# Attention with a routed FFN: the last 64 keys move from a chunk's thirteenth slot to its eighth

## The chip, the cores and the metric

One Trainium2 chip, one of its cores. The metric is the device time of the whole program in microseconds (us); a kernel's time is the median of its runs.

## The reference

Eight batches of 3136 tokens. `z` has 64 columns, `u` and `v` have 256.

```python
scores = scale * np.matmul(z, z.transpose(0, 2, 1))     # 8 x 3136 x 3136, scale = 1/3136
attn = np.maximum(scores, 0.0) ** 2
x = u * np.matmul(attn, v)
...
scores = np.einsum('bsd,d->bs', x, w_gate)
top_idx = np.argpartition(-scores[b], capacity)[:capacity]   # 128 tokens of each batch
h = np.maximum(x[b, top_idx] @ w1, 0.0)
out[b, top_idx] = x[b, top_idx] + sigmoid(scores[b, top_idx]) * (h @ w2)
```

The attention is nearly all of the work. Its scores are symmetric: the square for query i and key j is also the one for query j and key i.

## The kernel before

**Tiling.** The queries of a batch go in seven chunks: five of 512, one of 256, one of 320 (`chunks_of`, line 32). The keys are 24 tiles of 128 and a rest of 64. A chunk is worked off in 13 slots (`SLOTS`, line 108): twelve **pair slots** of two key tiles, and one **rest slot** for the 64 last keys. The list `slots` (lines 319 to 338) holds all 8 x 7 x 13 of them in the order in which they run. A pair is *new* when its scores are computed, or *old* when its squares are fetched, transposed, from an earlier chunk that computed them; old and new pairs are spread evenly over a chunk. Before the change the rest slot is the thirteenth of every chunk.

**A slot's work.** Values are split into a high and a low part of type fp32r, so that a product takes several matmuls. For a new pair, `scores` (line 426) issues four score matmuls on PE into one of two PSUM buffers (`sc`, line 440), a ReLU and a square on ACT (L450, the tile `a`; L451, the tile `hi`), and another full square of `a`, on DVE (L462) or on ACT (L456), as counters of estimated busy time choose. `low` (line 466) transposes the squares on DVE for later chunks (L483, L503) and makes the low part `lo` on POOL or DVE (L518), by the same counters. For an old pair ACT makes the high part from the fetched tile `qk` (L418), and the low part is again L518. The rest slot has two score matmuls, half the ACT work, and three short DVE operations on 64 partitions (L462, L474, L483); its high and low parts share one tile.

`mix` (line 526) then multiplies: a pair slot issues twelve matmuls (eight with `hi`, four with `lo`, line 556), a rest slot four with `hi` and `Vr`. They add up in two PSUM banks `acc`, one for each half of the 256 columns of `v`. There are three such banks, so a chunk's second half takes the bank that held the first half of the chunk before. In between, after `turn` matmuls, `mix` calls `more_scores(k + LEAD)`: scores are issued three slots ahead.

**The order.** Each engine's instructions run in the order in which the code issues them. At an edge between chunks stands `finish` (line 594): two DVE operations (L601) read the two banks and so release them; the transposes of the result, a product on POOL (L622) and a sum on DVE follow in later slots. The slot ahead of a rest slot issues its scores after four matmuls, not eight, and only squares the scores (`square_scores`) where it otherwise also makes the low parts; the rest of its work is held to the next slot (lines 1502 to 1505). The first slot of a chunk is sorted by half, so that the second half's bank is needed late (line 549). Routing and FFN of a batch run as tasks in the chunks of the next one.

**Loads.** All large transfers are issued from SP's queue in program order: fetches of old squares (`fetch`, lines 377 to 398; two pairs each, into one of three `qk` tiles, seven slots ahead of their use, lines 1338 to 1346), the next batch's `v` (`stage_v`, line 279), stores of squares and of the result. In the last chunk of a batch ACT and POOL also split the next batch's `v` into its parts (`prep_v`, line 294, L125 and L126), at slots fixed from the end of the batch (lines 1321 to 1330).

Of the kernel before, what the change touches and what calls it, by code (L numbers as in the profile page):

```python
# [25 lines left out]
LATE = 4  # L26
# [62 lines left out]
def attention_then_routed_ffn(ctx: ExitStack, tc: tile.TileContext, zt, ut, v, wg, w1, w2, cst, cst16, keys, outs, at, cap):  # L89
    nc = tc.nc  # L90
    B, S, D = v.shape
# [4 lines left out]
    NCH = len(CHUNKS)  # L96
    WHOLE = NCH - 2
    NK = D // P
    NJ = S // P
# [6 lines left out]
    ROUNDS = 32 // BITS  # L106
    SHARES = P >> BITS
    SLOTS = NJ // 2 + 1

    const = ctx.enter_context(tc.tile_pool(name="const", bufs=1))  # L110
    vpool = ctx.enter_context(tc.tile_pool(name="vpool", bufs=NJ // 2))
# [107 lines left out]
    V = {}  # L219
# [96 lines left out]

    slots = []
    for b in range(B):  # L320
        for c in range(NCH):
            known = min(c, WHOLE) * GT + (2 if c > WHOLE and b < B - 1 else 0)
            old = [(2 * g, 2 * g + 1) for g in range(known // 2)]
            new = [(2 * g, 2 * g + 1) for g in range(known // 2, NJ // 2)]
            if c == WHOLE and b < B - 1:
                new.reverse()
            if c < WHOLE and (b or c):

                new.insert(len(new) - 2, new.pop(1))
            wait = 0.5 if (b, c) == (0, 1) else 0.0  # L330
            both = [(wait + (1 - wait) * (i + 0.5) / len(old), 0, js, True) for i, js in enumerate(old)]
            place = [(i + 0.5) / len(new) for i in range(len(new))]
            if b < B - 1 and c == NCH - 1:
                place = [1.6 / len(old)]
            both += [(x, 1, js, False) for x, js in zip(place, new)]
            slots += [(b, c, js, is_old) for _, _, js, is_old in sorted(both)]
            slots.append((b, c, (NJ,), False))
    assert len(slots) == B * NCH * SLOTS

    squares = [  # L340
# [25 lines left out]
    near = deque()  # L366
# [159 lines left out]
    def mix(k, beside, between):  # L526
# [2 lines left out]
        b, c, js, _ = slots[k]  # L529
        assert k in parts  # L530
        hi, lo = parts.pop(k)
        first, last = k % SLOTS == 0, js[0] == NJ
        if first:
            acc[b, c] = [ps_a.tile([P, CH], F32, name="acc", tag="acc")[:, : CHUNKS[c][1]] for _ in range(NK)]
        ac = acc[b, c]
        todo = []
        if last:
            for h in range(NK):
                for w in range(2):
                    todo.append((h, V[b, NJ][:, w, h], hi[:, 0], w == 1))  # L540
        else:
            for h in range(NK):
                for q, j in enumerate(js):
                    for w in range(2):
                        todo.append((h, V[b, j][:, w, h], hi[:, q], False))
            for q, j in enumerate(js):
                for h in range(NK):
                    todo.append((h, V[b, j][:, 0, h], lo[:, q], False))
            if first and (b or c):
                todo.sort(key=lambda x: x[0])  # L550
        turn = (6 if c else 4) if first else 4 if last or len(slots[min(k + 1, len(slots) - 1)][2]) == 1 else 8
        done, lead, started = 0, 2, set()
        for n, (h, w, mov, stop) in enumerate(todo):
            if n == turn:
                between()
            nc.tensor.matmul(ac[h], w, mov, start=first and h not in started, stop=stop)  # L556
            started.add(h)
            upto = len(beside) * max(0, n - lead + 1) // (len(todo) - lead)
            for op in beside[done:upto]:
                op()  # L560
            done = max(done, upto)
        if turn == len(todo):
            if last:
                near.extend(finish(b, c))
            between()

    gate = {}
# [882 lines left out]
    for k, (b, c, js, is_old) in enumerate(slots):  # L1450
# [48 lines left out]
        now = settle_scores  # L1499
        posts = [*posts[:half], now, *posts[half:]]  # L1500
        held_posts = []
        if k + 2 < len(slots) and len(slots[k + 1][2]) == 1:

            now = square_scores if c < WHOLE and (b or c) else settle_scores
            posts, held_posts = [now], [fn for fn in posts if fn is not settle_scores]
# [9 lines left out]
        clock += took  # L1515
        if tasks:
            ready = max(told + 0.5, clock + 2.0)
        if len(js) == 1 and cap > 0:
            if c == NCH - 1 - late:
                far.extend([None, *route(b)])  # L1520
            elif c >= NCH - late:
# [64 lines left out]
```

## Time and profile before

| | |
|---|---|
| three runs, median (range) | 2067.78 us (2067.12 to 2067.83) |
| the profiled execution's own time | 2067.41 us |
| its span | 2065.6 us |
| PE busy | 2055.2 us (99%) |
| weight loads (PEld) busy | 1744.5 us (84%) |
| DVE, ACT, POOL busy | 1529.0 us (74%), 1291.2 us (63%), 1357.5 us (66%) |
| DMA share of the busiest queue | 70.9% |

The span runs from the first to the last instruction; the profiled execution's time is 1.8 us more than that. Matmuls are pipelined, and their ends are modelled: a row of PE shows 0.39 us for a matmul, while the next one starts 0.23 us later. So PE's busy share tells little; what tells is the distance between the starts of matmuls, and the waits of the weight loads that go ahead of them, which the profile lists apart as PEld.

### The profile page before, as it was taken

What the parts mean: (1) busy time and instruction counts of PE and PEld (TensorE: products, weight loads), DVE (VectorE), ACT (ScalarE), POOL (GpSimd) and SP (SyncE); (2) the same over time, 40 slices, a digit from 0 to 9 for tenths busy, and PEclk for the clock granted to TensorE, in tenths of its full rate; (3) what the DMA queues carried; (4) which work ended last, traced back from release to release, by engine and by line L of the source; (5) the groups of instructions that cost most, each with busy time, mean ns of one, the idle gap of its engine ahead of it and who ended that gap; (6) DMA issues with size and microseconds to landing.
All of it is one profiled execution on the core that took longest, in us unless ns stands there. A gap on an engine that the chain in (4) does not pass through costs nothing.

```text
span 2065.6 us, 31660 instructions
## 1 busy us (share of the span) xinstructions
PE 2055.2 (99%) x10280; PEld 1744.5 (84%) x10280; DVE 1529.0 (74%) x2667; ACT 1291.2 (63%) x1629; POOL 1357.5 (66%) x728
## 2 busy tenths in 40 slices
PE   9999999999999999999999999999999999999999
PEld 6888988889888898888988889888898888888788
DVE  7676678856788667875678756887578876787776
ACT  7665576656775467664676546765477654775543
POOL 6766587756876468764677647875578755765643
PEclk9999999999999999999999999999999999999999
DMA  6788767886668765787767877678776776666862
GB/s 197 207 232 226 217 188 207 233 231 190 193 188 232 212 205 177 199 233 210 208 185 193 235 203 217 184 192 236 194 222 188 192 201 178 206 192 164 213 173 95
DMA packets 442758, 415.52 MB, mean 201 GB/s; under 512 B 133792, under 2 KB 374880, under 8 KB 439520
## 3 DMA queue, kind: packets, MB, share of 16 engines
q1 hardware_dynamic: 441456, 411.01, 70.9%
q0 software_dynamic: 768, 2.10, 0.3%
q8 instruction: 80, 1.31, 0.3%
q14 instruction: 86, 0.70, 0.1%
q10 hardware_dynamic: 368, 0.39, 0.1%
HBM read 238.78 MB, written 174.60 MB: 200 GB/s over the span
## 4 chain that ended last, share of the span: by engine, by line
PE 87%; DVE 3%; issue 2%; ACT 2%; DMA 2%; POOL 1%; SPq 1%; POOLq 0%; DVEq 0%; ACTq 0%
PE acc L556 73%; PE sc L440 12%; ACT hi L451 1%; POOL lo L518 1%; ACT a L450 1%; DVE a L462 1%; DVE aT L483 1%; PE h L1215 1%; PE y L1259 1%; DMA vst<-in_v 0%; DMA squares<-aT 0%; DVE lo L518 0%; DMA qk<-in_zt 0%; PE spread L680 0%; DMA qk<-squares_narrow 0%
## 5 line engine op out<-in xcount | busy, mean ns | idle before, releaser
L556 PE MATMUL acc<-hi,V 128*128 128x512 f32 (+2 forms) x5376 | 1218.4, 364 | 0.5
L518 POOL TENSOR_TENSOR lo<-a,hi 128x1024 fp32r<-128x1024 f32 (+2 forms) x326 | 717.9, 2204 | 563.5 <-DVE a L462 426.7
L556 PEld LDWEIGHTS acc<-hi,V 128*128 128x128 f32 x5376 | 932.9, 188 | 157.4 <-DVE ut L601 5.5
L556 PE MATMUL acc<-lo,V 128*128 128x512 f32 (+2 forms) x2688 | 664.0, 363 | 1.0 <-POOL lo L518 1.0
L450 ACT ACTIVATE a<-sc 128x1024 f32<-128x1024 f32 (+4 forms) x401 | 358.2, 893 | 449.2 <-PE sc L440 421.0
L556 PEld LDWEIGHTS acc<-lo,V 128*128 128x128 f32 x2688 | 471.1, 188 | 76.7 <-POOL lo L518 4.4
L462 DVE TENSOR_TENSOR a<-sc,a 128x1024 f32<-128x1024 f32 (+5 forms) x306 | 307.4, 1005 | 249.8 <-ACT hi L451 225.8
L418 ACT CAST hi<-qk 128x1024 fp32r<-128x1024 f32 (+2 forms) x327 | 279.7, 860 | 220.1 <-PE acc L556 198.1
L483 DVE STREAM_TRANSPOSE aT<-a 128x512 f32<-128x512 f32 (+3 forms) x541 | 349.5, 681 | 76.7 <-ACT a L456 54.4
L451 ACT ACTIVATE hi<-a 128x1024 fp32r<-128x1024 f32 (+4 forms) x401 | 372.2, 928 | 24.8 <-PE acc L556 2.3
L518 DVE TENSOR_TENSOR lo<-qk,hi 128x1024 fp32r<-128x1024 f32 (+2 forms) x220 | 319.2, 1459 | 81.7 <-ACT hi L418 79.3
L440 PE MATMUL sc<-Z,ZH 128*128 128x512 f32 (+2 forms) x746 | 275.1, 373 | 2.3 <-DVE a L462 2.1
L440 PE MATMUL sc<-Z,ZL 128*128 128x512 f32 (+2 forms) x746 | 273.3, 370 | 0.1
L518 POOL TENSOR_TENSOR lo<-qk,hi 128x1024 fp32r<-128x1024 f32 (+2 forms) x107 | 210.0, 1965 | 51.3 <-ACT hi L418 41.6
L440 PEld LDWEIGHTS sc<-Z,ZH 128*128 128x128 f32 x746 | 140.5, 188 | 31.7 <-DVE a L462 6.0
L440 PEld LDWEIGHTS sc<-Z,ZL 128*128 128x128 f32 x746 | 140.5, 188 | 24.7 <-DVE ZL L126 0.5
L126 POOL TENSOR_TENSOR V<-vst,V 128x512 fp32r<-128x512 f32 x92 | 136.5, 1489 | 29.8 <-ACT V L125 26.4
L622 POOL TENSOR_TENSOR ut<-x,w_run 128x1024 f32<-128x1024 f32 (+2 forms) x52 | 126.0, 2422 | 24.4 <-DVE x L613 23.4
L456 ACT ACTIVATE a<-a 128x1024 f32<-128x1024 f32 x93 | 98.8, 1062 | 2.9
L126 POOL TENSOR_TENSOR ZL<-zst,ZH 128x512 fp32r<-128x512 f32 (+2 forms) x56 | 84.2, 1508 | 2.5 <-ACT ZH L125 2.2
L125 ACT CAST V<-vst 128x512 fp32r<-128x512 f32 x95 | 57.9, 609 | 35.5 <-DMA vst<-in_v 35.5
L601 DVE SCALAR_TENSOR_TENSOR ut<-acc,ut 128x512 f32<-128x512 f32 (+2 forms) x112 | 63.9, 611 | 19.5 <-PE acc L556 19.2
(187 smaller groups left out, 1083.1 us busy)
## 6 DMA issues: line engine op xcount, KB each, us to landing
squares<-aT SPq DMA_DIRECT2D x160, 512.0 KB
qk<-squares SPq DMA_DIRECT2D x320, 256.0 KB
squares_narrow<-aT SPq DMA_DIRECT2D x320, 128.0 KB
qk<-squares_narrow SPq DMA_DIRECT2D x80, 512.0 KB
out<-x SPq DMA_DIRECT2D x162, 128.0 KB
ut<-in_ut SPq DMA_DIRECT2D x40, 512.0 KB
vst<-in_v SPq DMA_DIRECT2D x158, 128.0 KB
squares_own<-aT SPq DMA_DIRECT2D x39, 256.0 KB
```

The source lines that it names most:

```text
L126: (lo_on or nc.vector.tensor_tensor)(lo, src, hi.bitcast(F32), op=ALU.subtract)
L418: nc.scalar.copy(by(hi), src)
L440: nc.tensor.matmul(ps[:, q], z[:, j * P : (j + 1) * P], mov, start=z is ZH, stop=z is ZL)
L450: nc.scalar.activation(a, ps[:, :n], AF.Relu)
L451: nc.scalar.activation(pieces[0][0](hi), pieces[0][1], AF.Square)
L456: nc.scalar.activation(a, a, AF.Square)
L462: square = lambda: nc.vector.tensor_tensor(a[rows], of[rows, :n], a[rows], op=ALU.mult)
L483: nc.vector.transpose(to, a[rows, q].rearrange("p (m t a) -> p m t a", m=GT, a=Q))
L518: on.tensor_tensor(view(lo), src, view(hi).bitcast(F32), op=ALU.subtract)
L556: nc.tensor.matmul(ac[h], w, mov, start=first and h not in started, stop=stop)
L601: nc.vector.scalar_tensor_tensor(xT[:, h, :w], acc[b, c][h], SCALE * SCALE, xT[:, h, :w], op0=ALU.mult, op1=ALU.mult)
L622: nc.gpsimd.tensor_tensor(wx, runs, consts["wg_run"].rearrange("p (o r) -> p o r", o=1).broadcast_to([P, NB, RUN]), op=ALU.mult,)
```

## The change

In chunks other than a batch's first, and other than the last batch's four last ones (`inside`), the rest slot is put in as the eighth of thirteen; a pair slot is then the last. So 44 of the 56 chunks change. The code that asked for "a rest slot" where it meant "the last slot of a chunk" now asks for the place. A last slot that is a pair has its matmuls sorted by half, as the first slot has (four with `hi` and two with `lo` of half one, then those of half two), and `finish` is called behind its twelfth matmul. Ahead of a rest slot that lies inside a chunk, the work after the slot is no longer cut down to squaring.

```diff
--- before.py
+++ after.py
@@ -106,6 +106,7 @@
     ROUNDS = 32 // BITS
     SHARES = P >> BITS
     SLOTS = NJ // 2 + 1
+    MIDDLE = SLOTS // 2 + 1
 
     const = ctx.enter_context(tc.tile_pool(name="const", bufs=1))
     vpool = ctx.enter_context(tc.tile_pool(name="vpool", bufs=NJ // 2))
@@ -316,6 +317,10 @@
 
 
 
+    def inside(b, c):
+
+        return c > 0 and c < (NCH if b < B - 1 else NCH - LATE)
+
     slots = []
     for b in range(B):
         for c in range(NCH):
@@ -333,8 +338,9 @@
             if b < B - 1 and c == NCH - 1:
                 place = [1.6 / len(old)]
             both += [(x, 1, js, False) for x, js in zip(place, new)]
-            slots += [(b, c, js, is_old) for _, _, js, is_old in sorted(both)]
-            slots.append((b, c, (NJ,), False))
+            mine = [(b, c, js, is_old) for _, _, js, is_old in sorted(both)]
+            mine.insert(MIDDLE if inside(b, c) else len(mine), (b, c, (NJ,), False))
+            slots += mine
     assert len(slots) == B * NCH * SLOTS
 
     squares = [
@@ -529,15 +535,15 @@
         b, c, js, _ = slots[k]
         assert k in parts
         hi, lo = parts.pop(k)
-        first, last = k % SLOTS == 0, js[0] == NJ
+        first, last, rest = k % SLOTS == 0, k % SLOTS == SLOTS - 1, js[0] == NJ
         if first:
             acc[b, c] = [ps_a.tile([P, CH], F32, name="acc", tag="acc")[:, : CHUNKS[c][1]] for _ in range(NK)]
         ac = acc[b, c]
         todo = []
-        if last:
+        if rest:
             for h in range(NK):
                 for w in range(2):
-                    todo.append((h, V[b, NJ][:, w, h], hi[:, 0], w == 1))
+                    todo.append((h, V[b, NJ][:, w, h], hi[:, 0], last and w == 1))
         else:
             for h in range(NK):
                 for q, j in enumerate(js):
@@ -545,10 +551,10 @@
                         todo.append((h, V[b, j][:, w, h], hi[:, q], False))
             for q, j in enumerate(js):
                 for h in range(NK):
-                    todo.append((h, V[b, j][:, 0, h], lo[:, q], False))
-            if first and (b or c):
+                    todo.append((h, V[b, j][:, 0, h], lo[:, q], last and q == 1))
+            if first and (b or c) or last:
                 todo.sort(key=lambda x: x[0])
-        turn = (6 if c else 4) if first else 4 if last or len(slots[min(k + 1, len(slots) - 1)][2]) == 1 else 8
+        turn = (6 if c else 4) if first else 4 if rest or len(slots[min(k + 1, len(slots) - 1)][2]) == 1 else 8
         done, lead, started = 0, 2, set()
         for n, (h, w, mov, stop) in enumerate(todo):
             if n == turn:
@@ -559,9 +565,9 @@
             for op in beside[done:upto]:
                 op()
             done = max(done, upto)
+        if last:
+            near.extend(finish(b, c))
         if turn == len(todo):
-            if last:
-                near.extend(finish(b, c))
             between()
 
     gate = {}
@@ -1499,7 +1505,7 @@
         now = settle_scores
         posts = [*posts[:half], now, *posts[half:]]
         held_posts = []
-        if k + 2 < len(slots) and len(slots[k + 1][2]) == 1:
+        if k + 2 < len(slots) and len(slots[k + 1][2]) == 1 and not inside(b, c):
 
             now = square_scores if c < WHOLE and (b or c) else settle_scores
             posts, held_posts = [now], [fn for fn in posts if fn is not settle_scores]
@@ -1515,7 +1521,7 @@
         clock += took
         if tasks:
             ready = max(told + 0.5, clock + 2.0)
-        if len(js) == 1 and cap > 0:
+        if k % SLOTS == SLOTS - 1 and cap > 0:
             if c == NCH - 1 - late:
                 far.extend([None, *route(b)])
             elif c >= NCH - late:
```

A rest slot in the middle changes the counters that choose engines. Over the whole program 23 squares go from ACT to DVE (L456: 93 before, 70 now; L462 with 128x1024: 186 before, 209 now), and some low parts change between POOL and DVE.

**PE at the edge between two batches.** The last chunk's slots have 320 columns, the next batch's first chunk 512; `Vr` is the part of `v` of the last 64 keys. Before, the end of the fourth batch:

```order
L440 MATMUL sc<-Z,ZL 128x512
L556 MATMUL acc<-lo,V 128x320 x4
L556 MATMUL acc<-hi,V 128x320 x4
L440 MATMUL sc<-Z,ZH 128x512
L440 MATMUL sc<-Z,ZL 128x512
L440 MATMUL sc<-Z,ZH 128x512
L440 MATMUL sc<-Z,ZL 128x512
L556 MATMUL acc<-hi,V 128x320 x4
L556 MATMUL acc<-lo,V 128x320 x4
L556 MATMUL acc<-hi,Vr 128x320 x4
L440 MATMUL sc<-Z,ZH 128x512
```

The same edge in the changed kernel:

```order
L446 MATMUL sc<-Z,ZL 128x512
L562 MATMUL acc<-lo,V 128x320 x4
L562 MATMUL acc<-hi,V 128x320 x8
L446 MATMUL sc<-Z,ZH 128x512
L446 MATMUL sc<-Z,ZL 128x512
L446 MATMUL sc<-Z,ZH 128x512
L446 MATMUL sc<-Z,ZL 128x512
L562 MATMUL acc<-lo,V 128x320 x4
L562 MATMUL acc<-hi,V 128x320 x4
L562 MATMUL acc<-lo,V 128x320 x2
L562 MATMUL acc<-hi,V 128x320 x2
L446 MATMUL sc<-Z,ZH 128x512
```

The first row of each is the end of the scores of the next chunk's first pair. Behind the last row shown come three more score matmuls and the edge, in the changed kernel with four more `acc` matmuls between them. So from the first row to the edge stood 20 `acc` matmuls and two groups of four score matmuls; now it is 28 and two. The second group, of the second pair, has 16 `acc` matmuls behind it where it had 12. The matmuls of the last slot come half by half.

**ACT in a batch's last chunk.** `V<-vst` splits the next batch's `v`, `Z<-ZH` and `Z<-ZL` prepare queries, `hi<-qk` is the high part of an old pair. Before:

```order
L125 CAST V<-vst 128x512
L271 CAST Z<-ZH 64x512
L271 CAST Z<-ZL 64x512
L418 CAST hi<-qk 128x2x320
L125 CAST V<-vst 128x512
L418 CAST hi<-qk 128x2x320 x2
```

Now:

```order
L126 CAST V<-vst 128x512
L272 CAST Z<-ZH 64x512
L272 CAST Z<-ZL 64x512
L424 CAST hi<-qk 128x2x320
L126 CAST V<-vst 128x512
L424 CAST hi<-qk 128x2x320 x2
```

The order on ACT stays. On PE the four `Vr` matmuls now stand ahead of the tenth slot, which uses the `hi` that follows the casts of `Z`; before, that slot had nine pair slots ahead of it, and now eight and the rest slot.

**SP's queue at the start of that chunk.** `squares_narrow_3` and `_4` are the sources of the fourth and the fifth fetch of the chunk, `vst` is the next batch's `v`. Before:

```order
L394 DMA qk<-squares_narrow_2_113 128x4x256
L397 DMA qk<-squares_narrow_2_113 128x256
L394 DMA qk<-squares_narrow_3_115 128x4x256
L397 DMA qk<-squares_narrow_3_115 128x256
L288 DMA vst<-in_v 32x4x256 x4
L394 DMA qk<-squares_narrow_4_117 128x4x256
L397 DMA qk<-squares_narrow_4_117 128x256
L288 DMA vst<-in_v 32x4x256 x4
```

Now:

```order
L400 DMA qk<-squares_narrow_2_113 128x4x256
L403 DMA qk<-squares_narrow_2_113 128x256
L289 DMA vst<-in_v 32x4x256 x4
L400 DMA qk<-squares_narrow_3_115 128x4x256
L403 DMA qk<-squares_narrow_3_115 128x256
L400 DMA qk<-squares_narrow_4_117 128x4x256
L403 DMA qk<-squares_narrow_4_117 128x256
L289 DMA vst<-in_v 32x4x256 x4
```

The fourth fetch goes out a slot later, behind the first load of `v`.

## Rows read from the trace of the kernel before

**Rows 1.** Page, span and section 1: busy time of each engine

```profile
span 2065.6 us, 31660 instructions
...
PE 2055.2 (99%) x10280; PEld 1744.5 (84%) x10280; DVE 1529.0 (74%) x2667; ACT 1291.2 (63%) x1629; POOL 1357.5 (66%) x728
```

**Rows 2.** Waits of PEld, 250 to 1815 us: total, times, longest

```profile
PEld acc L556 <- DVE ut L601: 4.1, 9, 0.5
PEld acc L556 <- POOL lo L518: 3.9, 11, 1.1
PEld sc L440 <- DVE a L462: 3.0, 9, 0.7
```

**Rows 3.** Timeline (start, us, what), PE, second batch, entry to third chunk

```profile
346.45 0.39 PE L440 MATMUL sc<-Z,ZH 128*128 128x512 f32 x1
...
347.35 1.07 PE L556 MATMUL acc<-hi,V 128*128 128x512 f32 x4
349.12 0.73 PE L556 MATMUL acc<-lo,V 128*128 128x512 f32 x2 [0.69 <-POOL lo L518]
```

**Rows 4.** Timeline of PE, fifth batch, entry to its first chunk

```profile
1024.66 1.08 PE L556 MATMUL acc<-hi,V 128*128 128x512 f32 x4
1025.61 0.50 PE L440 MATMUL sc<-Z,ZH 128*128 128x512 f32 x1
...
1026.64 0.63 PE L556 MATMUL acc<-lo,V 128*128 128x512 f32 x2
1027.33 1.19 PE L556 MATMUL acc<-hi,V 128*128 128x512 f32 x4
1028.35 0.61 PE L556 MATMUL acc<-lo,V 128*128 128x512 f32 x2
```

**Rows 5.** Timeline of DVE at the same entry

```profile
1024.33 1.23 DVE L462 TENSOR_TENSOR a<-sc,a 128x1024 f32<-128x1024 f32 x1
1025.59 1.31 DVE L483 STREAM_TRANSPOSE aT<-a 128x512 f32<-128x512 f32 x2
1026.82 0.85 DVE L601 SCALAR_TENSOR_TENSOR ut<-acc,ut 128x320 f32<-128x320 f32 x2
```

**Rows 6.** Timeline of PE, fourth batch, last chunk

```profile
1013.75 1.34 PE L556 MATMUL acc<-hi,V 128*128 128x320 f32 x8
1014.93 0.75 PE L556 MATMUL acc<-lo,V 128*128 128x320 f32 x4
1015.63 1.43 PE L556 MATMUL acc<-hi,V 128*128 128x320 f32 x8
```

**Rows 7.** Timeline of DVE, fourth batch, end of the second chunk

```profile
852.38 0.69 DVE L462 TENSOR_TENSOR a<-sc,a 64x512 f32<-64x512 f32 x1
...
853.72 0.71 DVE L483 STREAM_TRANSPOSE aT<-a 64x512 f32<-64x512 f32 x1
```

**Rows 8.** Timeline of POOL at the same place

```profile
855.76 2.40 POOL L518 TENSOR_TENSOR lo<-a,hi 128x1024 fp32r<-128x1024 f32 x1 [3.60 <-DVE a L462]
```

**Rows 9.** Groups by form, square on DVE: xcount, busy us, mean ns

```profile
L462 DVE TENSOR_TENSOR a<-sc,a 128x1024 f32<-128x1024 f32 x186 | 227.3, 1222 | 191.5 <-ACT hi L451 169.3 <-issue 20.9
```

**Rows 10.** Busy us (instructions), fourth batch, second chunk: PE PEld DVE ACT POOL

```profile
814.60:857.20 42.60, 42.60 (x191) 35.28 (x190) 40.53 (x98) 29.70 (x32) 29.86 (x15) 1.00 0.58 171
```

**Rows 11.** Timeline of DVE, fourth batch, middle of the second chunk

```profile
834.10 0.84 DVE L814 STREAM_TRANSPOSE ge<-own 32x32 f32<-32x32 f32 x4
```

**Rows 12.** Timeline of ACT, fourth batch, last chunk

```profile
1013.06 0.62 ACT L125 CAST V<-vst 128x512 fp32r<-128x512 f32 x1 [2.26 <-DMA vst<-in_v]
...
1014.85 0.73 ACT L418 CAST hi<-qk 128x640 fp32r<-128x640 f32 x1
```

**Rows 13.** Timeline of SP's queue, start of that chunk

```profile
1001.18 1.76 SPq L288 DMA_DIRECT2D vst<-in_v  x4
```

**Rows 14.** Groups by form: the low of 128x640 on POOL

```profile
L518 POOL TENSOR_TENSOR lo<-qk,hi 128x640 fp32r<-128x640 f32 x12 | 23.5, 1970 | 0.0
...
L518 POOL TENSOR_TENSOR lo<-a,hi 128x640 fp32r<-128x640 f32 x9 | 14.2, 1577 | 47.9 <-DVE a L462 42.5 <-PE old L1065 5.4
```

## Prediction, made before the changed kernel ran

> **What bounds the kernel now.** The page comes first: PE is busy 2055.2 us of a span of 2065.6 [rows 1]. The other engines have a quarter of their time free or more, so PE's own stream sets the end, and moving work among them pays only where PE stops. The reader should not conclude from 99% that only 10 us are to be had: a matmul's row is longer than its distance to the next. So I read the waits of the weight loads next. Between 250 and 1815 us, that is in batches two to seven and at the entries to batches two to eight, they name three things that PE waits for: the release of an `acc` bank by L601, 4.1 us in 9 waits; a low part from POOL, 3.9 us in 11; and the square on DVE that frees a score buffer, 3.0 us in 9 [rows 2]. All three would be small change in another kernel; here they are what is left.
>
> The timeline of PE shows what a wait costs the stream. The pace is four matmuls of 512 columns in 0.90 us, 0.226 each (346.45 to 347.35). In the second batch's third chunk the first `lo` matmul was due at 347.35 + 0.90 = 348.25 and starts at 349.12: 0.87 us lost [rows 3]. At the entry to the fifth batch the scores that start at 1025.61 take until 1026.64, 1.03 us for four: 0.13 lost. The second half's first matmul was due at 1026.64 + 0.45 = 1027.09 and starts at 1027.33, and its four take 1.02 instead of 0.90: 0.24 + 0.12 = 0.36 lost [rows 4]. Both places are the first slot of a chunk, right behind a rest slot.
>
> **The change, part by part.** No matmul is added or removed, so the sum is made of stops that go and stops that come.
>
> *Bank release.* DVE ran the second pair's square at 1024.33, its transposes at 1025.59, and only then L601, at 1026.82 [rows 5]. In the new order the scores of the next chunk's first two pairs are issued eight and four `acc` matmuls earlier before the edge (the order of PE above), 1.2 and 0.6 us at 0.147 us for 320 columns (eight in 1.18 us, from 1013.75 to 1014.93) [rows 6]. ACT takes the first pair, then the second, so DVE's chain starts about 1.0 us earlier. L601 then starts near 1025.8 and its first half is done 0.43 later, 1026.2; the bank is needed ten matmuls into the chunk, 1024.66 + 2.26 = 1026.9. The wait goes, with 0.7 us to spare. Nine waits at 0.36: **-3.2 us**.
>
> *Scores at the entry to a batch.* They wait for the same square, which now ends 1.0 us earlier. One such stop at each of seven entries, 0.13 each, with a little for longer ones: **-1.1 us**.
>
> *First low part.* At the end of the second chunk DVE does the rest slot's three operations, from 852.38 to 854.43, directly ahead of the square on which the first pair's low part rests [rows 7]; POOL's low part, 2.40 us, starts at 855.76 [rows 8]. These 2.05 us now lie half a chunk earlier, and the pair's scores are issued eight matmuls, 1.8 us, earlier. The longest wait in the list is 1.1 us, so all go. Of a wait of 1.1 the stream lost 0.87 and about 0.12 for the restart, that is 0.1 to 0.15 less than the wait: 3.9 - 11 x 0.15 = **-2.2 us**.
>
> *The last slot sorted by half.* Its low part is needed after four of its matmuls, where it would be eight and four scores without the sorting. Its scores are issued three slots ahead: 4 + 16 + 12 + 4 = 36 matmuls, 8.1 us. DVE's square takes 1.22 [rows 9] and POOL's low part 2.40 [rows 8], which leaves 4.5 for ACT's two passes and for queues. I cost it at nothing; ACT's slack covers it, and if DVE is late by more than 2 us it turns into the same wait as above.
>
> *The middle of a chunk.* The slot behind the rest slot has 1.8 us less from its scores to its use (a rest slot is 4 matmuls, a pair 12). The hardest place is the second chunk, where DVE is busy 40.53 of 42.60 us [rows 10]. There DVE ends a routing step at 834.10 + 0.84 = 834.94 [rows 11]; with the rest slot's ops next, their `hi` is complete 1.4 us later, 836.3. PE comes to the rest slot after 84 `acc` and 22 score matmuls, 814.6 + 106 x 0.226 = 838.6: 2.3 us to spare. The 23 squares that go to DVE cost it 23 x 1.22 = 28 us in 2065 [rows 9], under cover of its idle quarter. Bounds for the 37 middles outside the batches' last chunks: nothing below, since there was no stop to remove, and 0.87 each above [rows 3]. By the 2.3 us of room I take the lower end, 0.5 us in all: **+0.5 us**.
>
> *A batch's last chunk.* Here PE is fast, 0.147 us for a matmul. ACT waits until 1013.06 for the next batch's `v`, casts it, prepares `Z`, and only then, at 1014.85, copies the tenth slot's `hi`, ready at 1015.58 [rows 12]. PE was due there at 1014.93 + 0.59 = 1015.52 and started at 1015.63; with the restart 0.2 us lost [rows 6]. Now PE is there earlier, by a pair slot (12 x 0.147 = 1.76) less the rest slot (0.59) and its two scores (0.29): 0.88 us. If `v` lands as before, the stop grows by 0.88. But SP issued that chunk's first load of `v` at 1001.18, behind the fourth fetch [rows 13]; in the new queue it goes ahead of it (the order of SP above), which brings the chain of transfers forward by up to that fetch. Ends: 0 and 0.88 us for each of seven chunks. I take 0.2, nearer the end at which the load's new place pays: **+1.4 us**.
>
> Sum: -3.2 - 1.1 - 2.2 + 0.5 + 1.4 = -4.6 us, against the profiled execution's own 2067.41: 2062.8. The median of the runs shown, 2067.78, is 0.37 above that execution, so the forecast for a median is **2063.2 us**.
>
> **The rivals.** *A, the forecast:* the edges come free and the middles hold, 2060.5 to 2065.
>
> *B, given back in the last chunk:* the tenth slot's `hi` is late by the full 0.88 in seven chunks, 6.2 us, against the gain of 6.5: 2067.5. For it speaks that ACT takes its queue in order and stood 2.26 us before that cast [rows 12]; against it the new place of the load.
>
> *C, slower:* in that same chunk the next slot is late too. Its low part moves to POOL behind a second part of `v`; it takes 1.58 to 1.97 us there [rows 14], where the slot gives eight matmuls, 1.18 us, from `hi` to `lo`: 0.4 to 0.8 more. With 0.88 + 0.8 = 1.68 in seven chunks, 11.8 - 6.5 = +5.3: 2073.1. It decides from 6.5 + 4.1 = 10.6 us of new stops, 1.5 us a batch. At 1.58 us for the low part it would be 1.28 a batch and 2070.3, no longer slower by what can be measured. Which of the two holds, the rows show in part: the same shape takes 1.97 us when its source is `qk`, in slots where DVE makes other low parts, and 1.58 when it is `a` [rows 14]. The Trainium skill (GPSIMD Engine Reference, Key points) says that GpSimd shares its SBUF interfaces with VectorE and is held up by vector instructions with two SBUF inputs, which DVE's low parts are. By that rule the longer price holds and C is 2073.1; the two rows agree with it, but do not show the overlap itself.
>
> *D, the edges stay late:* the squares and low parts that the counters now give to DVE stand ahead of L601 and of the first low part, so that only half of the 6.5 goes: 3.2 - 1.9 = 1.3 us gained, 2066.5. For it speaks the second chunk's full DVE [rows 10]; against it that most of what moves lands in chunks with room.
>
> **How the numbers follow.** A 0.2% difference, 4.1 us, is about what a measurement of this kernel can tell from no change. A has 0.52; the greater part of its span lies beyond -4.1 (below 2063.6), so 0.45 of it counts as faster and 0.07 as the same. B has 0.26, all the same. C has 0.14, slower. D has 0.08, the same. Together: faster 0.45, same 0.41, slower 0.14. The range reaches from 2060.0, where all three stops go and nothing comes (6.5 us, and a little at the edges of batches one and eight), to 2071.5, which takes in B, D and C's lower price and leaves out C itself and the tails, under 0.2. A's own range is 2060.5 to 2065.
>
> **What would show it.** Right: the waits of the weight loads for L601 and for POOL's low part fall from 4.1 and 3.9 us to under 1 each, and the starts at the entries to batches keep the pace of 0.226. B and C show as waits for ACT's `hi` (L418 before) or a low part in each batch's last chunk, with ACT idle for `v`; D as L601 waits that stay near 4. New waits in the slot behind the rest slot in chunks two to five would prove my middles wrong. The forecast is wrong if the time lies above 2065.

## The result, and the profile after

The changed kernel takes 2081.39 us (median of 6 runs, 2080.80 to 2082.95), the kernel before 2067.74 in the same comparison (6 runs, 2067.12 to 2068.33): ratio 1.0067, 95% interval 1.0054 to 1.0080. I forecast 2063.2 us and a range up to 2071.5; the change costs 13.7 us.

The page of the changed kernel, span and section 1, against [rows 1]:

```profile
span 2079.7 us, 31583 instructions
...
PE 2057.5 (99%) x10280; PEld 1744.9 (84%) x10280; DVE 1618.1 (78%) x2707; ACT 1267.8 (61%) x1606; POOL 1325.0 (64%) x711
```

The span is 14.1 us longer with the same matmuls. DVE is busy 89 us more. The 23 squares at 1.22 us are 28 of them, and 17 low parts that POOL made before are some 27. Most of what is left is the same number of operations taking longer: the rest slots' `hi` 13 us, the scans (L894) and an addition (L919) of the routing 9 us each.

The waits of the weight loads in the same stretch as [rows 2] (total us, times, longest):

```profile
PEld L902 <- issue: 6.1, 6, 1.5
PEld L942 <- DVE of L936: 4.2, 6, 0.7
PEld acc L562 <- ACT hi L424: 3.7, 6, 1.3
PEld acc L562 <- DVE ut L607: 3.1, 8, 0.7
PEld acc L562 <- POOL lo L524: 3.0, 11, 0.4
PEld h L1221 <- DVE xs L127: 2.6, 5, 1.0
```

And PE's own waits there:

```profile
PE ahead L901 <- DVE upto L894: 4.5, 6, 1.2
PE acc L562 <- ACT hi L424: 2.1, 5, 1.0
PE taken L942 <- DVE of L936: 1.7, 6, 0.3
```

New at the top are L901 and L942, small matmuls of the routing of the batch before, which run in PE's stream. They stop it in six batches, in the third chunk and at its end. What was to go did go at the places that the forecast named; the L607 waits and the waits for POOL's `lo` that the list still has, 3.1 and 3.0 us, are at others. The timeline of PE at the entry to the fifth batch, which answers [rows 4]:

```profile
1030.69 1.09 PE L562 MATMUL acc<-hi,V 128*128 128x512 f32 x4
1031.62 0.39 PE L446 MATMUL sc<-Z,ZH 128*128 128x512 f32 x1
...
1032.53 0.62 PE L562 MATMUL acc<-lo,V 128*128 128x512 f32 x2
1032.99 1.09 PE L562 MATMUL acc<-hi,V 128*128 128x512 f32 x4
1033.92 0.62 PE L562 MATMUL acc<-lo,V 128*128 128x512 f32 x2
```

Four scores from 1031.62 to 1032.53 are 0.91 us, two `lo` 0.46: no stop is left. Nor is one at the entry to the second batch's third chunk [rows 3], where the `lo` that waited 0.69 us now follows four `hi` in 0.90:

```profile
347.15 1.07 PE L562 MATMUL acc<-hi,V 128*128 128x512 f32 x4
348.05 0.61 PE L562 MATMUL acc<-lo,V 128*128 128x512 f32 x2
```

For an account by place I took the distance of every matmul of these three widths to the next start, less the pace (0.227 us for 512 columns, 0.147 for 320, 0.120 for 256), and added up what is over 0.02. It is an account of the one profiled execution of a kernel. The sum is 25.2 us before and 39.2 now, a difference of 14.0, which is the span's. The last column is the best kernel of the runs below.

| us of stops of PE | before | changed | e11 |
|---|---|---|---|
| entries to batches two to eight | 3.7 | 0.0 | 0.0 |
| entries to third chunks | 2.6 | 0.1 | 0.1 |
| entries to fifth chunks | 0.6 | 0.2 | 0.2 |
| third chunk, around L901 | 0.5 | 6.3 | 0.5 |
| its end, around L942 | 0.5 | 3.2 | 0.5 |
| rest of the fourth chunk (L1221, low parts, L607) | 0.4 | 4.2 | 0.4 |
| sixth chunk | 0.0 | 3.7 | 0.0 |
| last chunk, tenth slot | 0.7 | 3.9 | 0.4 |
| last chunk, else | 0.7 | 0.9 | 1.0 |
| eighth batch, third chunk | 0.2 | 2.2 | 1.6 |
| all else (the program's start and end among it) | 15.2 | 14.7 | 13.9 |

The first three rows are the gain, 6.6 us; the forecast said 6.5. The rows below them are 21 us of new stops, where it had 1.9. Of the 3.7 us in the sixth chunk, 1.5 are in the first batch alone.

**What is late in the third chunk.** Timelines of PE, DVE and POOL, fourth batch, changed kernel:

```profile
893.95 1.07 PE L562 MATMUL acc<-lo,V 128*128 128x512 f32 x4
895.69 0.16 PE L901 MATMUL ahead<-upto,c 98*98 98x2 bf16 x1 [0.67 <-DVE upto L894]
...
892.75 2.89 DVE L894 TENSOR_TENSOR_SCAN upto<-mk 98x32 bf16<-98x32 bf16 x2
...
900.07 1.74 DVE L919 TENSOR_TENSOR ahead<-quota,taken 98x1 f32<-98x1 f32 x1
...
893.17 2.38 POOL L524 TENSOR_TENSOR lo<-qk,hi 128x1024 fp32r<-128x1024 f32 x1
...
899.39 2.39 POOL L524 TENSOR_TENSOR lo<-qk,hi 128x1024 fp32r<-128x1024 f32 x1
```

The same place in the kernel before:

```profile
886.40 2.10 DVE L518 TENSOR_TENSOR lo<-qk,hi 128x1024 fp32r<-128x1024 f32 x1
...
888.63 1.22 DVE L888 TENSOR_TENSOR_SCAN upto<-mk 98x32 bf16<-98x32 bf16 x2
...
892.89 0.17 DVE L913 TENSOR_TENSOR ahead<-quota,taken 98x1 f32<-98x1 f32 x1
...
887.38 2.28 POOL L126 TENSOR_TENSOR ZL<-zst,ZH 128x512 fp32r<-128x512 f32 x1
889.70 2.41 POOL L518 TENSOR_TENSOR lo<-a,hi 128x1024 fp32r<-128x1024 f32 x1
...
890.17 0.17 PE L895 MATMUL ahead<-upto,c 98*98 98x2 bf16 x1
```

An addition of 98 numbers takes 1.74 us, and ends at 901.81, where POOL's low part ends (899.39 + 2.39 = 901.78). The two scans (running counts of chosen tokens) take 2.89 us and end at 895.64, where another low part ends (893.17 + 2.38 = 895.55). Before, the scans ended at 889.85, 0.32 ahead of PE. Now PE was due at 893.95 + 4 x 0.227 = 894.86, 0.78 too early; with the 1.22 us of before the scans would have ended at 893.97. DVE did not come late to them: it started the scans 1.54 us ahead of PE's 890.17 before, and 2.11 us ahead of 894.86 now. And in the kernel before, the first scan was long already: the second starts at 889.66 (its row stands at the end), 1.03 us behind the first, where POOL's L126 ends (887.38 + 2.28). I had three theories. *O:* the rest slot's three operations on DVE, 2.05 us [rows 7], now stand ahead of the routing, which comes late. *K:* the counters gave DVE more squares and low parts. *P:* operations of DVE wait for whole operations of POOL.

### The profile page after: what moved, and what is told of

Read it like the earlier page. It is cut to its first block, busy times and chain, and to the rows that moved or that the text cites. A ratio compares the mean times of both kernels' runs of the same rounds, so it can differ in the third digit from the quotient of the medians.

```text
span 2079.7 us, 31583 instructions
## 1 busy us (share of the span) xinstructions
PE 2057.5 (99%) x10280; PEld 1744.9 (84%) x10280; DVE 1618.1 (78%) x2707; ACT 1267.8 (61%) x1606; POOL 1325.0 (64%) x711
## 4 chain that ended last, share of the span: by engine, by line
PE 76%; DVE 10%; DMA 5%; issue 3%; ACT 2%; SPq 2%; POOL 1%; POOLq 0%; DVEq 0%; ACTq 0%
PE acc L562 62%; PE sc L446 12%; DVE aT L489 2%; DVE a L468 2%; DVE lo L524 2%; DMA qk<-squares 1%; DMA out<-x 1%; DMA qk<-squares_narrow 1%; POOL lo L524 1%; PE h L1221 1%; PE y L1265 1%; ACT a L456 1%; SPq L626 1%; DMA qk<-in_zt 1%; ACT hi L424 1%
## 5 line engine op out<-in xcount | busy, mean ns | idle before, releaser
L524 POOL TENSOR_TENSOR lo<-a,hi 128x1024 fp32r<-128x1024 f32 (+2 forms) x310 | 701.5, 2265 | 566.9 <-DVE a L468 359.9
L456 ACT ACTIVATE a<-sc 128x1024 f32<-128x1024 f32 (+4 forms) x401 | 358.4, 894 | 444.4 <-PE sc L446 423.0
L468 DVE TENSOR_TENSOR a<-sc,a 128x1024 f32<-128x1024 f32 (+5 forms) x329 | 335.2, 1019 | 197.3 <-ACT hi L457 171.6
L127 POOL TENSOR_TENSOR V<-vst,V 128x512 fp32r<-128x512 f32 x92 | 130.5, 1424 | 17.6 <-ACT V L126 14.1
L127 POOL TENSOR_TENSOR ZL<-zst,ZH 128x512 fp32r<-128x512 f32 (+2 forms) x56 | 72.8, 1305 | 22.1 <-ACT ZH L126 22.1
L462 ACT ACTIVATE a<-a 128x1024 f32<-128x1024 f32 x70 | 74.4, 1064 | 2.2
L607 DVE SCALAR_TENSOR_TENSOR ut<-acc,ut 128x512 f32<-128x512 f32 (+2 forms) x112 | 65.1, 610 | 13.1 <-PE acc L562 12.9
L126 ACT CAST V<-vst 128x512 fp32r<-128x512 f32 x95 | 58.1, 611 | 21.5 <-DMA vst<-in_v 21.5
```

Source lines behind the costliest of these rows:

```text
L127: (lo_on or nc.vector.tensor_tensor)(lo, src, hi.bitcast(F32), op=ALU.subtract)
L456: nc.scalar.activation(a, ps[:, :n], AF.Relu)
L462: nc.scalar.activation(a, a, AF.Square)
L468: square = lambda: nc.vector.tensor_tensor(a[rows], of[rows, :n], a[rows], op=ALU.mult)
L524: on.tensor_tensor(view(lo), src, view(hi).bitcast(F32), op=ALU.subtract)
L607: nc.vector.scalar_tensor_tensor(xT[:, h, :w], acc[b, c][h], SCALE * SCALE, xT[:, h, :w], op0=ALU.mult, op1=ALU.mult)
```

## The experiments

Unless it says otherwise an edit is made in the changed kernel. Each time stands beside runs of the kernel before on the same chip: 2067.75 for e1 and e3 to e5, 2068.56 for e6 to e9, 2067.73 for e10 to e13.

### e1: the rest slot stays last in the third chunk

```diff
-        return c > 0 and c < (NCH if b < B - 1 else NCH - LATE)
+        return c > 0 and c != 2 and c < (NCH if b < B - 1 else NCH - LATE)
```

> The rest slot stays last in every third chunk; all else is as in the changed kernel. Theory O (the place of the rest slot in the third chunk makes TensorE stop there at L901 and L942, together about 9 us in six batches, and in the following chunk about 3.6 us more): the stops of the third chunk go and most of those of the fourth, the first low part of the third chunk stays on time; 2069 to 2072.5 us. Rival K (the counters now give VectorE more squares and low parts everywhere, and the stops only move to the next full chunk): 2077 us or more.

Measured 2068.0 us, ratio 1.0 (0.9991 to 1.0009), 1 us below theory O's range and far from K's. The third chunk's place alone costs 13.4 us: the stops around L901, L942 and in the fourth chunk are all back at their values of before (0.5, 0.5, 0.4), and the entry to the third chunk is still free. The sixth and last chunks keep theirs (5.4 and 4.4 us; the profiled execution took 2070.39 us, so these are above a median one's). The run does not tell O from P, for the scans and the addition are also back at their durations of before (0.19 us for the second scan, 0.17).

### e3 and e4: order and choice of engines exchanged

A table of the choices that one kernel's counters made is put in place of the counters in the other: in e3 the old choices in the changed kernel, in e4 the new choices in the kernel before.

```diff
-        if n == 2 and (2 <= k < 2 + LEAD or k > 1 and busy["act"] + 3 * act < busy["dve"] + dve + turned):
+        if n == 2 and not chosen(k, 0):
...
-                if busy["pool"] + took > busy["dve"] + dve + (1.2 if busy["pool"] > 0 else 0.0):
+                if chosen(k, 1 + i):
```

> The changed order, but each square and each low part goes to the engine that the kernel before chose for the same keys. Rival K (it is the 23 squares and the low parts that moved to VectorE): the stops at L901 and L942 go, 2068 to 2072 us. Theory O (the rest slot's three operations, 2.05 us, now stand ahead of the scan, which was ready 0.3 us before TensorE came): the third chunk keeps most of its stops, 2076 to 2082 us. Rival P (VectorE's scan and its 98x1 addition wait for a low part that GpSimd is in: 2.42 and 1.74 us instead of 0.6 and 0.17, ending with GpSimd's operation): depends on where GpSimd's low parts now fall, 2072 to 2082 us, and the two durations tell.

> The order of the kernel before, with each square and low part on the engine that the changed kernel chose for the same keys. Rival K: most of the loss comes back, 2073 us or more. Theory O and rival P: near the kernel before, 2066.5 to 2070 us, since TensorE's routing matmuls come where they came and VectorE's 3.3 us more in the third chunk lie partly behind the scan.

Measured 2091.83 us (e3, ratio 1.0118, 1.0103 to 1.0134) and 2092.19 (e4, 1.0123, 1.0107 to 1.0138). Both are 24 us slower than the kernel before. For e3 that is beyond what any theory had said; e4 lies in K's case, which had no upper end. Taken alone e4 speaks for K and e3 against it; together they show that order and choices belong together. The largest wait of the weight loads in e3, then PE's in e4, 250 to 1815 us:

```profile
PEld acc L579 <- POOL lo L541: 19.2, 20, 2.2
```

```profile
PE taken L953 <- DVE of L947: 15.5, 6, 2.6
```

In e3 a low part, half of which the counters had moved off POOL, is late there. The durations of the scans and of the addition (min/median/max ns), in e3 and then in e4:

```profile
L911 DVE TENSOR_TENSOR_SCAN upto<-mk x14: 197/1098/1298, 382.0 to 1882.4; 98x32 bf16<-98x32 bf16 x14
...
L936 DVE TENSOR_TENSOR ahead<-quota,taken x7: 168/168/169, 387.4 to 1888.8; 98x1 f32<-98x1 f32 x7
```

```profile
L905 DVE TENSOR_TENSOR_SCAN upto<-mk x14: 201/958/2431, 376.0 to 1882.6; 98x32 bf16<-98x32 bf16 x14
...
L930 DVE TENSOR_TENSOR ahead<-quota,taken x7: 168/1734/1736, 383.3 to 1886.2; 98x1 f32<-98x1 f32 x7
```

With the two kernels that makes four cases, in each of batches two to seven:

| order, choices | second scan, us | addition, us |
|---|---|---|
| old, old (before) | 0.19 | 0.17 |
| new, new (changed) | 2.39 to 2.42 | 1.73 to 1.74 |
| new, old (e3) | 1.30 | 0.17 |
| old, new (e4) | 2.42 to 2.43 | 1.73 to 1.74 |

So the addition is long with the new choices, in either order, and the scan longest: it is the changed choice of engines, more than the place of the rest slot, that puts POOL's low parts beside these two operations. Whether the wait for POOL is what costs the time, P, was left to be tried.

A part of the 24 us is TensorE's clock. In e3's trace the granted clock falls from 1.0 to 0.5 (2.4 to 1.2 GHz) twice in the middle of the program, in e4's four times, each time at the end of a stop of 1.9 to 2.8 us in the third chunk or within 1.6 us behind it; not every such stop is followed by one. In e3 the eight matmuls of 512 columns from 900.98 take until 904.09, 3.11 us instead of 1.82. No other run's trace shows such a fall between the program's start and its end.

### e5: two low parts on POOL left out

```diff
-                on.tensor_tensor(view(lo), src, view(hi).bitcast(F32), op=ALU.subtract)
+                if 0 < b < B - 1 and (c, js[0]) in ((2, 6), (3, 0)):
+                    lo = hi
+                else:
+                    on.tensor_tensor(view(lo), src, view(hi).bitcast(F32), op=ALU.subtract)
```

> The changed kernel, but in batches two to seven two low parts on GpSimd are left out, that of keys six and seven in the third chunk and that of the first keys in the fourth; the matmuls that used them take the high part in their place, so the output lacks those terms and TensorE's and VectorE's work stays what it was. They are the two that GpSimd is in while VectorE's scan takes 2.42 us and its 98x1 addition 1.74. Rival P: the scan falls to about 0.6 and the addition to about 0.2 us, the stops at L901 and L942 go nearly all, 9 us less: 2071.5 to 2074 us. Theory O and rival K (VectorE simply has too much to do ahead of the scan): its queue is as full as before, the stops stay, 2079 us or more.

Measured 2073.55 us, ratio 1.0033 (1.0022 to 1.0044): 7.8 us less than the changed kernel, with DVE's operations as before. The scans by form in the changed kernel (min/median/max ns), then here:

```profile
L894 DVE TENSOR_TENSOR_SCAN upto<-mk x14: 200/538/2423, 379.7 to 1871.9; 98x32 bf16<-98x32 bf16 x14
```

```profile
L897 DVE TENSOR_TENSOR_SCAN upto<-mk x14: 191/206/545, 379.7 to 1863.0; 98x32 bf16<-98x32 bf16 x14
```

The stops around L901 and L942 fall from 6.3 and 3.2 us to 0.7 and 0.5. P holds; O and K, by which DVE simply has too much to do and which wanted 2079 or more, fall as main causes.

### e6: all the work, with an operand in PSUM

```diff
+            mk = misc_bank("runs")[:R, : 2 * NT]
+            nc.vector.tensor_copy(mk, st["mk"])
...
-                nc.vector.tensor_tensor_scan(upto[:, part], st["mk"][:, part], st["mk"][:, part], 0.0, ALU.add, ALU.max)
+                nc.vector.tensor_tensor_scan(upto[:, part], mk[:, part], st["mk"][:, part], 0.0, ALU.add, ALU.max)
...
-            ties, before, begin = (own[:, i : i + 1] for i in range(3))
-            left, end = (ps[:, 8 + i : 9 + i] for i in range(2))
+            ties, before = (own[:, i : i + 1] for i in range(2))
+            left, end, begin = (ps[:, 8 + i : 9 + i] for i in range(3))
```

> The changed kernel with the same work done, but each of the two operations that GpSimd held up gets one operand in PSUM: VectorE first copies the masks to a bank (one small copy more) and scans from there, and the beginning of each range stands in the bank, so the 98x1 addition reads it there. The squares, which read one operand from PSUM, take 1.19 to 1.23 us whatever GpSimd does. Theory P (the lengthened operations read two operands from SBUF while GpSimd is in a low part): scans of 0.2 to 0.3 us and additions of 0.17, the stops at L901 and L942 go as they did when the two low parts were left out, 2072 to 2075 us. If instead the lengthening has nothing to do with where the operands are: 2079 us or more.

Measured 2075.63 us, ratio 1.0035 (1.0022 to 1.0048), 0.6 us above the case of P and 3.4 below the other; its runs spread from 2071.46 to 2080.19, and the profiled one took 2071.94. DVE and POOL in the third chunk of its fourth batch:

```profile
889.66 0.34 DVE L896 TENSOR_TENSOR_SCAN upto<-runs,mk 98x32 bf16<-98x32 f32 x2
...
893.02 1.48 DVE L915 TENSOR_TENSOR ahead<-quota 98x1 f32<-98x1 f32 x1
...
895.25 0.17 DVE L921 TENSOR_TENSOR ahead<-ahead,taken 98x1 f32<-98x1 f32 x1
...
889.72 2.40 POOL L524 TENSOR_TENSOR lo<-qk,hi 128x1024 fp32r<-128x1024 f32 x1
892.08 2.39 POOL L524 TENSOR_TENSOR lo<-a,hi 128x1024 fp32r<-128x1024 f32 x1
...
894.57 2.39 POOL L524 TENSOR_TENSOR lo<-qk,hi 128x1024 fp32r<-128x1024 f32 x1
```

The second scan (889.80) and the addition now take 0.20 and 0.17 us inside POOL's low parts, and so in all of batches two to seven. L915, whose two inputs I left in SBUF, still takes 1.48 and ends with POOL's operation (894.50 and 894.47). The stops are 0.7 and 0.5 us, as in e5. So what counts for these two operations is where the operands lie.

### e7, e8, e12: one kind of chunk at a time

The condition in `inside` is `c == NCH - 1 and b < B - 1` (e7, last chunks), `c in (1, 3)` with the bound on the last batch (e8, second and fourth), `c == WHOLE and b < B - 1` (e12, sixth).

> The kernel before, with the rest slot in the middle of the batches' last chunks alone (and last slots sorted by half). Theory L (the forecast's rival B: in that chunk the tenth slot's high part stands on ScalarE behind a cast that waits for the next batch's v, so TensorE stops there for 4 to 4.5 us in seven batches, as much as the 3.5 us that the entries to the batches gain): 2066.5 to 2069.5 us, with stops for ACT's hi and none for L607 at the entries. Rival K (those stops come from the shifted choices of engines in the chunks ahead): 2063 to 2065.5 us.

> The rest slot in the middle in the second and fourth chunks alone. These free the third chunk's first low part (2.5 us) and the one L607 wait at the entry to some fifth chunks (0.8 us) and leave the third, sixth and last chunks, where the stops came, as they were. If the gains and losses of single chunks add up: 2063.5 to 2066 us. If the counters shift other chunks' work, as they did in the run with old choices: 2067 us or more.

> The kernel before, with the rest slot in the middle in the sixth chunks alone. If what single chunks cost adds up: the changed kernel's 2081.4, less 13.4 for the third chunk, is 2068.0; the second and fourth chunks gave 2.9 and the last ones cost 0 net, so the sixth chunks (and the fifth) cost about 2.8 us; with stops for a low part near its end, 2069 to 2071 us. If they cost only in the changed kernel's own shift of choices: 2067 to 2068.3 us.

Measured 2068.47 us (e7, ratio 1.0, 0.9991 to 1.0009), 2065.64 (e8, 0.9985, 0.9976 to 0.9994) and 2069.92 (e12, 1.001, 1.0001 to 1.0019). Single chunks add up: 13.4 for the third, -2.9 for the second and fourth, -0.1 for the last, 2.2 for the sixth make 12.6 of the 13.7; the fifth chunk was not tried alone. In e7's profiled execution, at 2070.34 us 1.9 above the median, the entries give back 3.5 us and the tenth slot costs 6.2 more (0.7 to 6.9).

### e9: the last slot not sorted by half

```diff
-            if first and (b or c) or last:
+            if first and (b or c):
```

> The changed kernel without the sorting of the last slot by halves. The last slot's low part is then needed four matmuls later, so the stops for it at the end of the sixth chunk (2.5 us in seven) go; the first half of a bank is complete four matmuls later, 0.6 to 0.9 us, against the 0.7 us to spare that I worked out at the entries. If the sorting does little for the entries: 2079 to 2081 us. If the entries need it: the L607 waits come back there, 0.1 to 0.4 us in each of some forty chunks, 2083 to 2090 us.

Measured 2083.08 us, ratio 1.007 (1.0057 to 1.0084). It lies at the edge of the second case, but not for its reason: the entries to batches and to third chunks stay free (0.0 and 0.1 us), and the sixth chunk keeps 3.3 us. The table differs from the changed kernel's by some 1 us in a row at most, as in the rest of the last chunk (1.9 against 0.9). The sorting hardly matters; it is not what frees the entries.

### e10, e11, e13: a version that keeps the gains

All three have the rest slot in the middle in the second, fourth and last chunks. e10 puts it in the eleventh place in the last chunk, e11 issues the loads of `v` a slot earlier, e13 does both.

```diff
-            mine.insert(MIDDLE if inside(b, c) else len(mine), (b, c, (NJ,), False))
+            mine.insert((10 if c == NCH - 1 else MIDDLE) if inside(b, c) else len(mine), (b, c, (NJ,), False))
...
-                load = (k - (3 if b else 2), lambda b=b, g=g: stage_v(b, g // 2))
+                load = (k - (4 if b else 2), lambda b=b, g=g: stage_v(b, g // 2))
```

> The rest slot in the middle in the second and fourth chunks, and in the batches' last chunks in the eleventh place, behind the tenth slot, whose high part was the one late with the rest slot ahead of it. Theory L: TensorE comes to the tenth slot when it came before the change, so its stops there stay at 0.1 to 0.2 us each, and the entries to the batches (0.53 us each in seven) are free all the same: 2061 to 2063.5 us. If the eleventh slot's parts are late in its place, or the entries need the full distance: 2065 to 2067 us.

> The rest slot in the middle in the second, fourth and last chunks, and each of the next batch's loads of v issued one slot earlier, ahead of the fetch that SyncE waits at. Theory L (ScalarE's cast of v, which waits for that load, stands ahead of the tenth slot's high part): the stops for the high part in the last chunk, 6.2 us in the run with the last chunk alone, go or fall under 2 us; 2061 to 2064 us. If v is slow for the transfers beside it and not for its place in the queue, or another thing holds ScalarE: the stops stay, 2065 to 2068.5 us.

> The eleventh place in the last chunk and the earlier loads of v together, with the rest slot in the middle in the second and fourth chunks. Theory L: either alone removes the stop at the tenth slot; together also the 0.2 us that the kernel before lost there: 2060.5 to 2063 us. Rival: the earlier loads collide with other transfers: 2064 us or more.

Measured 2064.53 us (e10, ratio 0.9985, 0.9976 to 0.9994), 2061.82 (e11, 0.9972, 0.9961 to 0.9982) and 2061.62 (e13, 0.997, 0.9958 to 0.9982). The waits of the weight loads in e11, in the stretch of [rows 2], are all of this:

```profile
PEld L942 <- issue: 1.6, 6, 0.3
PEld acc L562 <- POOL lo L524: 0.9, 6, 0.2
```

e11 is some 6 us faster than the kernel before and 20 faster than the change. e10 came out between its cases: the tenth slot is free, but the rest slot behind it waits in its place, 0.1 to 0.6 us in each batch. e11 has no wait for ACT's `hi` left in that stretch; a run with its places of the rest slot and without its earlier loads was not made, so what the loads do by themselves rests on e7 beside it. e13 is no better than e11 by what can be measured.

## Why the prediction was wrong

**Bank release, scores at the entries, first low part (-3.2, -1.1, -2.2): right**, at the places they were about: 6.6 us of stops went, against 6.5. Rival D did not come there, although DVE has more to do. My sign for it, waits for L607 and for POOL's `lo` under 1 us each, was not met (3.1 and 3.0): in six batches L607 is now late at the entry to the fourth chunk, 0.2 us of stops each, behind the long addition. In e5 and e6 these stops are gone.

**The last slot sorted by half (0): right**, by e9, as far as the noise tells.

**The middle of chunks (+0.5): the step that failed.** By the account it came to some 18 us (the third chunk and its end, the fourth, the sixth, and the eighth batch). I had set its upper bound at 0.87 us for each of 37 middles, 32 us, and took the lower end after looking at one thing, whether the rest slot's `hi` is ready when PE comes to the slot; it is. Two things were left out. PE's stream holds small matmuls of the routing that wait for DVE, with 0.32 us to spare; the sum needed a term for each. And the price of the shifted choices, "23 squares under cover of DVE's idle quarter", took DVE's time as a sum of its own durations, where two operations last longer when POOL is in a low part. The work put ahead on DVE did not make them late by itself: DVE started the scans earlier than before, measured against PE, and with the scans at 1.22 us there would have been no stop. What made the stop is where POOL's low parts came to lie: e5 and e6 take away 7.8 and 5.8 us in the median, and the same stops. That the changed choices, more than the order, put them there is the reading of e3 and e4; the two were not tried apart without other stops beside them. The sign that I had named for a wrong middle, waits in the slot behind the rest slot, did not come: the stops are at the twelfth slot and at the chunk's end.

Most of the rest of the 13.4 us is in the fourth chunk. Of its 3.8 us of stops more, the 1.2 for L607 at its entry go in e5 and e6; the others, for L1221 and a low part, stay (2.7 in e6) or grow (4.7 in e5), so they have another cause, which stays open. In the eighth batch a gathered tile lands 2 us after PE is due. That stop is there without the third chunk's new place (1.6 us in e1) and with the second and fourth chunks alone (1.7 in e8), and not in e7 and e12; it was not taken apart further.

In the prediction I weighed the Trainium skill (GPSIMD Engine Reference, Key points) only for POOL held up by DVE. That section of the Trainium skill names contention with VectorE's instructions of two SBUF inputs, and does not say which of the two waits. The Trainium skill (SBUF — State Buffer, section "SBUF: two separate sides") says more: of a VectorE operation with two SBUF inputs and a GpSimd operation that reads SBUF, the one that starts first has the shared ports for its whole length and the other waits. The rows agree with it. In e6 an operation with two SBUF inputs lasts 1.48 us, to POOL's end, and one with an input in PSUM takes 0.17. And POOL waits too: its L126 at 887.38 takes 2.28 us beside DVE's low part (886.40, 2.10 us), and the shortest of the same form take 1.27 to 1.29 us.

**A batch's last chunk (+1.4): the right mechanism, too small.** Rival B's wait came at its place. ACT, then PE, sixth batch, changed kernel:

```profile
1531.76 0.62 ACT L126 CAST V<-vst 128x512 fp32r<-128x512 f32 x1 [2.34 <-DMA vst<-in_v]
...
1533.55 0.73 ACT L424 CAST hi<-qk 128x640 fp32r<-128x640 f32 x1
...
1532.59 0.75 PE L562 MATMUL acc<-lo,V 128*128 128x320 f32 x4
1534.33 0.85 PE L562 MATMUL acc<-hi,V 128*128 128x320 f32 x4 [0.99 <-ACT hi L424]
```

It costs 3.2 us more than before, 0.46 a batch on average, between my ends of 0 and 0.88; the sixth batch, shown, has the longest stop (1.25), the third the shortest (0.1). I had taken 0.2, for the new place of one load in SP's queue. In e7's profiled execution, without the other chunks' changes, it is the full 0.88 on average (6.2 in seven). In e11 the loads are issued one slot earlier and the stop is gone but for 0.4 us in the first batch, so the place in the queue does bear on it. Rival C did not come: the next slot's low part is on time.

**The sixth chunk: left out.** Its 3.7 us I had put under the middles at nothing. A fetch goes out seven slots ahead of its use; where one of the seven is a rest slot, that is eight matmuls less. At 0.120 us for a matmul that is 1.0 us. ACT, then POOL and PE, sixth batch:

```profile
1513.57 0.62 ACT L424 CAST hi<-qk 128x512 fp32r<-128x512 f32 x1 [1.94 <-DMA qk<-squares_narrow]
...
1514.27 1.29 POOL L524 TENSOR_TENSOR lo<-qk,hi 128x512 fp32r<-128x512 f32 x1 [2.54 <-ACT hi L424]
...
1515.62 0.75 PE L562 MATMUL acc<-lo,V 128*128 128x256 f32 x4
```

PE was due at 1514.48 + 8 x 0.120 = 1515.44, POOL ended at 1515.56. The fetch lost more than the 1.0 us, for it now stands behind the stores of the result in SP's queue. Changed kernel, sixth batch:

```profile
1506.67 2.44 SPq L626 DMA_DIRECT2D out<-x  x4
1509.22 0.71 SPq L400 DMA_DIRECT2D qk<-squares_narrow  x1
```

Kernel before, fourth batch:

```profile
987.38 0.82 SPq L394 DMA_DIRECT2D qk<-squares_narrow  x1
988.30 2.62 SPq L620 DMA_DIRECT2D out<-x  x4
```

It is so in all seven batches, and in e12 too; against the end of the chunk the fetch goes out 1.8 to 3.2 us later than before. That this is why the low part is late is read from the rows; no run moved the fetch back ahead of the stores.

## What to carry to other kernels

A change of order that shifts the choice of engines is not priced by adding up durations: look at every instruction of the bounding engine that waits for the engines concerned, small ones of other stages too, at the slack of each, and at what the operations it waits for would last beside another engine's work. Freeing an edge of 0.4 us is no gain if another matmul had 0.3 to spare and its operation grows by 1.7. Leads that are counted in slots shrink where a short slot comes to lie inside them, and a transfer that moves by one slot can change places with another in its queue. And a change to the order pays or not place by place: here two kinds of chunk gained, two lost, one needed an earlier load, and trying them apart turned a loss of 14 us into a gain of 6.

## What the runs showed of the hardware that was not expected

A VectorE operation with both inputs in SBUF can last as long as a GpSimd operation that started a moment before it, whatever its own size: 98 numbers took 1.74 us beside a low part of 2.4, and 0.17 without. The order of two starts decides, here by 0.04 us: in the kernel before the second scan starts 0.03 to 0.05 us ahead of POOL's low part in all of batches two to seven, in the changed kernel 0.04 to 0.05 behind it. The second scan in the fourth batch, in the kernel before, starts ahead of POOL's low part (889.70):

```profile
889.66 0.19 DVE L888 TENSOR_TENSOR_SCAN upto<-mk 98x32 bf16<-98x32 bf16 x1
```

In the changed kernel it starts behind POOL's (893.17):

```profile
893.21 2.42 DVE L894 TENSOR_TENSOR_SCAN upto<-mk 98x32 bf16<-98x32 bf16 x1
```

With one input in PSUM no row shows such a wait. The squares, which read `sc` there, have the mean of [rows 9] in the changed kernel too, and the longest takes 1.23 us, although 97 of the 209 lie beside a POOL operation for more than 0.6 us:

```profile
L468 DVE TENSOR_TENSOR a<-sc,a 128x1024 f32<-128x1024 f32 x209 | 255.3, 1221 | 161.1 <-ACT hi L457 138.4 <-issue 20.0 <-POOL lo L524 1.6
```
